# Output projection in an attention kernel: another set of seven products per four quadrants

## The chip, the cores and the metric

The kernel runs on one core of a Trainium2 chip. The core has a matrix engine (TensorE, "PE" in the profile, with its weight loads as "PEld"), a vector engine (VectorE, "DVE"), an activation engine (ScalarE, "ACT"), a general engine (GpSimd, "POOL") and a queueing engine (SyncE, "SP"). Transfers are issued from the queues of SP and ACT and carried by 16 DMA engines. The metric is device time in microseconds (us). The kernel before takes 888.16 us, the median of 3 runs (887.34 to 888.82).

## The reference

The input is `x`, 2048 rows of 640. It is layer-normed, and two branches work on the result.

- Branch A is attention with 32 heads of 192, over the last 512 positions of a K and a V cache: `q = xn @ wq`, a softmax over the scores, the weighted sum of V, and the output projection `o @ wo`, where `o` is 2048 x 6144 and `wo` is 6144 x 640.
- Branch B is a gated feed-forward: `(silu(xn @ w_gate) * (xn @ w_up)) @ w_down`, followed by another silu; call it `g`.

The result is `x + (o @ wo) * g`.

## The kernel before, in words

The program has three stages, written out by hand: each engine carries out its instructions in the order in which the code issues them (`tc.manual_schedule()`).

**First stage (0 to about 170 us).** Layer norm and branch B. `g` is stored to DRAM in `g_d`. Beside this, VectorE prepares `wo`: it is read in pieces (`wo_pieces`), sums of quadrants of it are formed in fp16 (`wo_sums`, L360) and stored to `wo_d` (L362).

**Second stage (about 170 to 698 us).** Attention, in 16 pairs of heads, about 33 us each. One pair is two halves; each half is a phase of scores (8 calls of `scores`, with the next q products between them) and a stretch of `pv`. ScalarE takes the exponential of each score tile (L651); score tiles have two buffers. V of a pair has one buffer, `V_p`, so its load (L181) can start only after the `pv` of the pair before, and the first `pv` of the new pair waits for it. The output of a pair is divided, transposed by DMA (L718) and stored to `o_d` in DRAM (L727). `beside(pr, n)` hangs further work at step `n` (0 to 15) of pair `pr`; the table `AHEAD` lists what is fetched for the third stage: `load_b` fetches the prepared operand of a product (always on ACT's queue here, L760, 128 x 7680 elements of 2 bytes), `load_a` fetches quadrants of `o`, and `wo_part` (L739, SP's queue) copies a bare quadrant of `wo` from DRAM to DRAM into `wo_d`, a quarter at a time, so that a later `load_b` reads it in long runs.

**Third stage (698 us to the end).** The output projection. Two row tiles of 128 make a row pair (`ROW_PAIRS`, 8 of them, number `n`). Per pair the left operand has four quadrants (two row tiles by two halves of the 6144), and `wo` has four (two halves of the 6144 by two halves of the 640 columns). The four result quadrants are formed from seven products instead of eight, by Strassen's method: `A_OF` and `B_OF` say which quadrants each product's operands are summed from. `a_sum` forms a sum on VectorE (L789); its three buffers rotate, two under the tag `qT` and one in the pool `late[0]`; the sum after next but one is issued after the product that used its buffer. `product` (L796) runs 24 matmuls of 128 x 320 into a PSUM bank. `run(n, m)` issues a product and then what takes its result out of PSUM: copies on ScalarE (L853, L868), sums on VectorE (`total`, L835), `finish` (L818, L819), which multiplies by `g` and adds `x`, and `store` (L823). `ORDER` runs the first two row pairs product by product in turn, and the other six one after the other. `load_xg` (L805, L806) fetches `x` and `g` of a pair. The loads and stores of this stage stand in SP's queue in program order.

Before the third stage starts, ACT's queue holds, in this order: the last divisions of the attention, one `load_b` (L760) into the pool `late[0]`, and then the first copies out of PSUM.

Of the kernel before, what the change touches and what calls it, by code (L numbers as in the profile page):

```python
# [10 lines left out]
ALU = mybir.AluOpType  # L11
# [4 lines left out]
def kernel(  # L16
# [66 lines left out]
    def mm_tile(which=None):  # L83
# [14 lines left out]
    M6, M3, M1, M5, M4, M2, M7 = PRODUCTS = range(7)  # L98
    A_OF = {
        M1: (0, 3, ALU.add), M2: (2, 3, ALU.add), M3: (0,), M4: (3,), M5: (0, 1, ALU.add),  # L100
        M6: (2, 0, ALU.subtract), M7: (1, 3, ALU.subtract),
    }
    B_OF = {
        M1: (B11, B22, ALU.add), M2: (B11,), M3: (B12, B22, ALU.subtract), M4: (B21, B11, ALU.subtract),
        M5: (B22,), M6: (B11, B12, ALU.add), M7: (B21, B22, ALU.add),
    }
    B_SUMS = [m for m in PRODUCTS if len(B_OF[m]) == 3]
    B_PARTS = [m for m in PRODUCTS if len(B_OF[m]) == 1]
# [3 lines left out]
    wo_d = dram.tile([len(PRODUCTS), P, KH, HC], h16, name="wo_d")  # L112
# [115 lines left out]
    with ExitStack() as fctx:  # L228
# [119 lines left out]
        def wo_sums(n, ks):  # L348

            t = won[n]  # L350
            if not ks.start:
                won["sums"] = ffw.tile([P, len(B_SUMS), 2, HC], h16, name="wo_s")
            sums = won["sums"]

            def piece(q):
                return t[:, q[0], :, q[1] * HC : (q[1] + 1) * HC]

            for k in ks:
                x, y, op = B_OF[B_SUMS[k]]
                nc.vector.tensor_tensor(sums[:, k, :, :], piece(x), piece(y), op)  # L360
            if ks.stop == len(B_SUMS):
                nc.sync.dma_start(  # L362
                    out=wo_d[0 : len(B_SUMS), :, 2 * n : 2 * n + 2, :].rearrange("s p c d -> p s c d"), in_=sums[:, :, :, :]
                )
# [371 lines left out]
    def wo_part(m, c0, c1):  # L736

        k, n = B_OF[m][0]
        nc.sync.dma_start(  # L739
            out=wo_d[len(B_SUMS) + B_PARTS.index(m), :, c0:c1, :].bitcast(bf),  # L740
            in_=wo[(k * KH + c0) * P : (k * KH + c1) * P, n * HC : (n + 1) * HC].rearrange(
                "(c p) d -> p c d", p=P
            ),
        )

    def load_b(m, pool=None, eng=nc.scalar):
        if m in b_w:
            pass
        elif pool is None:
            flat = xc[:, 0:3, :, :].rearrange("p s c n -> p (s c n)")  # L750
            b_w[m] = flat.bitcast(bf).rearrange("p (c d) -> p c d", d=HC)
        else:
            b_w[m] = b_tile(m, pool)[:, :, :]
        if eng is None:
            return
        if m in B_SUMS:
            src = wo_d[B_SUMS.index(m), :, :, :]
        else:
            src = wo_d[len(B_SUMS) + B_PARTS.index(m), :, :, :].bitcast(bf)
        eng.dma_start(out=b_w[m], in_=src)  # L760
# [22 lines left out]
    def a_sum(n, m):  # L783
        x, y, op = A_OF[m]
        third = len(a_s) % 3 == 2
        a_s[n, m] = (late[0] if third else qpool).tile(
            [P, KH, P], h16, name="a_s", tag="a_s" if third else "qT", bufs=1 if third else 2
        )
        nc.vector.tensor_tensor(a_s[n, m][:], a_q[n, x][:], a_q[n, y][:], op)  # L789
# [19 lines left out]
    NAMES = ("m3", "e1", "f1", "m4", "f2", "c21", "y0", "g1")  # L809

    def f_tile(name):
        return temps[:, NAMES.index(name), :]

    def finish(n, side, k, s):

        t, cols = xg[n, side], slice(k * HC, (k + 1) * HC)
        y = f_tile("y0")
        nc.vector.tensor_tensor(y, s, t[:, 1, cols], ALU.mult)  # L818
        nc.vector.tensor_tensor(t[:, 0, cols], y, t[:, 0, cols], ALU.add)  # L819
# [7 lines left out]
    IN_TURN = (M6, M3, M1, M5, M4, M2, M7)  # L827
    ORDER = [(n, m) for ms in ((M6, M3), (M1,), (M5,), (M4,), (M2,), (M7,)) for n in range(2) for m in ms]
    ORDER += [(n, m) for n in range(2, len(ROW_PAIRS)) for m in IN_TURN]
# [11 lines left out]
    def e1_tile(n):  # L841
        return f_tile("e1") if n % 2 == 0 else late[2][:, :]

    def run(n, m):

        ahead = n + 2 < len(ROW_PAIRS)
        if m == M6:
            product(n, M6, bank(n, "Y"))
        elif m == M3:
            Z = bank(n, "Z")  # L850
            product(n, M3, Z)
            acc[n, "m3"] = f_tile("m3" if n % 2 == 0 else "y0")
            nc.scalar.copy(acc[n, "m3"], Z)  # L853
        elif m == M1:
            S = bank(n, "S")
            product(n, M1, S)
            acc[n, "e1"] = e1_tile(n)
            total(acc[n, "e1"], S, acc[n, "m3"])
        elif m == M5:
            product(n, M5, acc[n, "Z"], first=False)  # L860
            acc[n, "f1"] = f_tile("f1" if n % 2 == 0 else "g1")
            total(acc[n, "f1"], acc[n, "e1"], acc[n, "Z"], ALU.subtract)
            finish(n, 0, 1, acc[n, "Z"])
        elif m == M4:
            X = bank(n, "X")
            product(n, M4, X)
            acc[n, "m4"] = f_tile("m4" if n % 2 == 0 else "m3")
            nc.scalar.copy(acc[n, "m4"], X)  # L868
            for q in (0, 2) if ahead else ():
                load_a(n + 2, q)  # L870
        elif m == M2:
            S = bank(n, "S")
            product(n, M2, S)
            f2, c21 = f_tile("f2"), f_tile("c21")
            total(f2, acc[n, "e1"], S, ALU.subtract)
            total(c21, S, acc[n, "m4"])
            total(f2, acc[n, "Y"], f2)
            finish(n, 1, 0, c21)
            finish(n, 1, 1, f2)
            store(n, 1)  # L880
            for q in (1, 3) if ahead else ():
                load_a(n + 2, q)
        else:
            X, f1, t = acc[n, "X"], acc[n, "f1"], xg[n, 0]
            product(n, M7, X, first=False)
            if (n, m) != ORDER[-1]:
                total(f1, X, f1)
                finish(n, 0, 0, f1)
                store(n, 0)
            else:  # L890
                total(f1, f1, t[:, 1, 0:HC], ALU.mult)
                total(f1, f1, t[:, 0, 0:HC])
                store(n, 0, slice(HC, D))
                total(f_tile("f2"), X, t[:, 1, 0:HC], ALU.mult)
                total(t[:, 0, 0:HC], f_tile("f2"), f1)
                store(n, 0, slice(0, HC), nc.scalar)
            if ahead:
                load_xg(n + 2)
# [20 lines left out]
    def beside(pr, n):  # L919
# [23 lines left out]
        (1, 10): (load_b, M6, pre), (4, 10): (load_b, M3, pre), (7, 10): (load_b, M1, pre),  # L943
# [5 lines left out]

    for k, m in enumerate(B_PARTS):  # L950
        for n in range(4):
            AHEAD[2 + 3 * k + n // 2, (7, 15)[n % 2]] = (wo_part, m, n * KH // 4, (n + 1) * KH // 4)
# [35 lines left out]
    load_b(M4, wide, None)  # L988
# [9 lines left out]
    for name in LAST.split():  # L998
# [7 lines left out]
        elif name == "2b1":  # L1006
            load_a(0, 3, new)
            load_a(1, 3, new)
            load_b(M4)
# [14 lines left out]
    late.append(late[0].tile([P, HC], f32, name="e1"))  # L1024
    load_b(M7, late[0], None)
    a_sum(*A_SUMS[2])
    load_b(M2, late[0])
    load_xg(0)
    load_xg(1)
    load_b(M7, eng=nc.sync)  # L1030
# [32 lines left out]
```

## Time and profile before

The profiled execution took 887.44 us, of which the span between the first and the last instruction is 885.6 us. The clock granted to TensorE is 1.0, full speed, throughout.

| | us |
|---|---|
| Median of 3 runs | 888.16 |
| Profiled execution / its span | 887.44 / 885.6 |
| TensorE busy, whole span | 875.5 (99%) |
| VectorE busy | 599.1 (68%) |
| ScalarE busy | 404.1 (46%) |
| TensorE busy from 698 to 881 us (third stage) | 182.92 of 183.00 |
| VectorE busy in the same stretch | 116.17 |
| DMA engines, mean busy share, in the same stretch | 0.57 |
| DMA engines, mean busy share, 170 to 698 us | 0.85 |

Busy time of TensorE counts matmuls whose ends are modelled, so the idle time of an engine between two instructions, and what ended it, tells more than the share. In a line of the timeline the columns are the start, the duration, the engine, the line of code, the operation, output and inputs, the count, and in brackets the idle time before it with what ended it. "SPq" and "ACTq" are a queue's own instructions: the time in which it hands over a transfer, not the transfer itself.

### The profile page before, as it was taken

The numbers are of one execution on the slowest core, as the hardware profiler recorded it, in microseconds if no ns is written. First come the engines' busy times: TensorE is split into PE (matmuls) and PEld (weight loads), VectorE is DVE, ScalarE is ACT, GpSimd is POOL, SyncE is SP. The second block draws the span as 40 slices with busy tenths as digits, with TensorE's granted clock in tenths as the row PEclk, the third lists the DMA queues.
The fourth block names the chain that finished last, engine by engine and source line by source line (L and its number), as shares of the span: only waits on it lengthen the run. The fifth ranks groups of instructions, "written<-read, shape, count | busy, mean of one in ns | idle before, by whom it ended". The sixth has DMA issues, their size and how long they took to land.

```text
span 885.6 us, 22930 instructions
## 1 busy us (share of the span) xinstructions
PE 875.5 (99%) x9705; PEld 581.0 (66%) x9705; DVE 599.1 (68%) x1020; ACT 404.1 (46%) x577; POOL 114.1 (13%) x215
## 2 busy tenths in 40 slices
PE   9999999999999999999999999999999999999997
PEld 6455555567667666766766766766766777777775
DVE  6464786177777776777867777877875467666664
ACT  4222222466666666666666666666667300000000
POOL 0000001012132132132132132132120000000000
PEclk9999999999999999999999999999999999999999
DMA  9669877247999979979878777979799998655420
GB/s 296 166 183 273 212 222 226 66 69 175 231 199 212 182 164 254 193 165 213 228 156 190 157 155 174 195 145 218 160 208 278 221 346 297 216 173 181 171 69 16
DMA packets 271494, 169.44 MB, mean 191 GB/s; under 512 B 174112, under 2 KB 266400, under 8 KB 270496
## 3 DMA queue, kind: packets, MB, share of 16 engines
q1 hardware_dynamic: 269456, 154.12, 72.3%
q10 hardware_dynamic: 1936, 13.86, 4.3%
q8 instruction: 76, 1.25, 0.6%
q14 instruction: 26, 0.21, 0.1%
HBM read 91.91 MB, written 44.17 MB: 154 GB/s over the span
## 4 chain that ended last, share of the span: by engine, by line
PE 95%; DMA 2%; DVE 2%; issue 1%; ACTq 0%; ACT 0%; SPq 0%
PE acc L796 19%; PE sc L647 18%; PE mm L593 12%; PE sc L369 11%; PE mm L686 10%; PE sc L686 9%; PE mm L579 8%; PE mm L390 6%; DMA V_p<-in_A_v_cache_dram 1%; PE mm L402 1%; DMA x_t<-in_A_x_dram 1%; PE gu L369 0%; DMA xnT<-xn 0%; DVE a_s L789 0%; DVE xc L835 0%
## 5 line engine op out<-in xcount | busy, mean ns | idle before, releaser
L651 ACT ACTIVATE p_t<-sc 128x1024 bf16<-128x1024 f32 x256 | 253.7, 1024 | 59.9 <-PE sc L647 55.5
L647 PE MATMUL sc<-qT,khat 64*128 64x512 bf16 x1536 | 198.0, 376 | 0.0
L686 PEld LDWEIGHTS <-p_t 64*128 64x128 bf16 x4096 | 172.8, 94 | 11.6 <-DMA V_p<-in_A_v_cache_dram 2.0
L647 PEld LDWEIGHTS <-khat 64*128 64x128 bf16 x1536 | 89.0, 94 | 75.1 <-issue 0.3
L796 PEld LDWEIGHTS <-a_s 128*128 128x128 f16 x960 | 93.8, 98 | 36.9 <-DVE a_s L789 0.6
L686 PE MATMUL mm<-V_p,p_t 64*128 64x193 bf16 x2112 | 112.2, 243 | 2.3 <-DMA V_p<-in_A_v_cache_dram 2.3
L796 PE MATMUL acc<-b_w,a_s 128*128 128x320 f16 (+1 forms) x768 | 107.1, 299 | 0.1
L686 PE MATMUL sc<-V_p,p_t 64*128 64x193 bf16 x1984 | 104.8, 243 | 0.0
L584 DVE TENSOR_REDUCE qT<-mm 128x512 bf16<-128x1024 f32 x66 | 80.6, 1223 | 29.7 <-PE mm L579 27.2
L593 PE MATMUL mm<-xc,wq_p 64*128 64x512 f16 x750 | 94.4, 376 | 0.0
L593 PEld LDWEIGHTS <-wq_p 64*128 64x128 f16 (+1 forms) x1050 | 58.6, 94 | 47.6
L631 POOL TENSOR_TENSOR m_f<-m_f 128x1024 f32<-128x1024 f32 x28 | 65.8, 2351 | 178.0 <-DVE qT L626 178.0
L715 ACT ACTIVATE O_b<-sc,r 128x192 bf16<-128x192 f32 x120 | 44.0, 420 | 89.7 <-PE sc L686 80.3
L579 PE MATMUL mm<-xnT,wq_p 64*128 64x512 bf16 x660 | 82.9, 376 | 0.5 <-DVE qT L584 0.5
L789 DVE TENSOR_TENSOR a_s<-a_q 128x3072 f16<-128x3072 bf16 x40 | 69.3, 1750 | 7.1 <-issue 7.1
L369 PE MATMUL sc<-xnT,wg_sb 128*128 128x512 bf16 (+1 forms) x260 | 60.2, 354 | 1.4 <-DMA xnT<-xn 1.1
L579 PEld LDWEIGHTS <-wq_p 64*128 64x128 bf16 x660 | 36.1, 94 | 36.8 <-issue 5.7
L369 PE MATMUL sc<-xnT,wu_sb 128*128 128x512 bf16 (+1 forms) x260 | 60.3, 354 | 0.0
L377 DVE TENSOR_TENSOR hT<-sc,sg 128x512 bf16<-128x512 f32 x46 | 31.5, 687 | 42.4 <-ACT sg L376 42.2
L376 ACT ACTIVATE sg<-sc 128x512 bf16<-128x512 f32 x46 | 27.3, 596 | 69.7 <-PE sc L369 69.7
L704 DVE RECIPROCAL r<-mm 128x4 f32<-128x4 f32 x66 | 12.0, 183 | 68.2 <-PE mm L686 68.1
L626 DVE TENSOR_TENSOR qT<-mm,m_f 128x1024 bf16<-128x1024 f32 x30 | 36.7, 1225 | 31.6 <-ACT m_f L623 31.6
(82 smaller groups left out, 860.3 us busy)
## 6 DMA issues: line engine op xcount, KB each, us to landing
o_d<-OT_b SPq DMA_DIRECT2D x64, 384.0 KB, 5.9
a_q<-o_d SPq DMA_DIRECT2D x28, 768.0 KB, 6.1
wo_d<-wo_s SPq DMA_DIRECT2D x12, 800.0 KB, 4.8
b_w<-wo_d ACTq DMA_DIRECT2D x5, 1920.0 KB, 9.9
won<-in_A_wo_dram SPq DMA_DIRECT2D x24, 320.0 KB, 5.4
wq_rows<-in_A_wq_dram SPq DMA_DIRECT2D x16, 480.0 KB, 4.6
wq_rows<-in_A_wq_dram SPq DMA_DIRECT2D x30, 240.0 KB, 6.0
K_p<-in_A_k_cache_dram SPq DMA_DIRECT2D x32, 192.0 KB, 6.7
```

Source lines behind the costliest of these rows:

```text
L369: nc.tensor.matmul(out, w_sb[:, c, f * P : (f + 1) * P], xnT[:, c, qc], start=(c == 0), stop=(c == NC - 1),)
L390: nc.tensor.matmul(dn[:, n, 0:HC], hTs[b][:, f, rows], wd_sb[:, f, n * HC : (n + 1) * HC], start=(f == 0), stop=(f == NF - 1),)
L579: nc.tensor.matmul(q_ps[:, h, :], w[r, AS_IS[j], c, :], xnT[r, c, b * 512 : (b + 1) * 512], start=(c == 0), stop=(c == NC - 1),)
L584: nc.vector.reduce_sum(q_of(i, j), q_ps[:, :, :].rearrange("p h n -> p n h"), axis=AX.X)
L593: nc.tensor.matmul(ps[:, h, :], ws[h][r, c, :], xs[h][r, c, :], start=(first and c == 0), stop=(c == NC - 1), skip_group_check=True,)
L631: eng.tensor_tensor(m_f[:, SIDE_S, :, :], diag, m_f[:, SIDE_S, :, :], ALU.subtract)
L647: nc.tensor.matmul(sc[:, h, :], khat[r, j, ks], q_of(i, j)[r, :], start=(j == 0), stop=(j == 2))
L651: nc.scalar.activation(p_t[:, :, :], sc[:, :, :], ACT.Exp, scale=scale)
L686: m = nc.tensor.matmul(acc[:, k, h * 256 : h * 256 + Dh + 1], Ps[i][kc][r, h, qt * P : (qt + 1) * P], V_p[r, kc, h, 0 : Dh + 1], start=(p ...
L715: nc.scalar.activation(O_b[:, qt, h, :], a_k[:, h, 0:Dh], ACT.Copy, scale=r[:, k, h, :])
L789: nc.vector.tensor_tensor(a_s[n, m][:], a_q[n, x][:], a_q[n, y][:], op)
L796: nc.tensor.matmul(ps[k] if ns > 1 else ps, at[:, c, :], b_w[m][:, c, k * w : (k + 1) * w], start=(first and c == 0), stop=(c == KH - 1), ...
```

## The change

The seven products are formed by another scheme with four operand sums on each side instead of five, where sums are built on one another: on the left A11-A21, A21+A22, (A21+A22)-A11 and A12-((A21+A22)-A11), and on the right likewise. The products are run in the order M1, M7, M2, M5, M6, M4, M3. Three of the four result quadrants are added up in PSUM: M2 is accumulated on M1's bank, M4 on M7's, M3 on M5's, after the first product's value has been copied or summed out of the bank (M1 and M7 by a copy on ScalarE, M5 by a sum on VectorE). Bare quadrants of `wo` are now the right operands of three products, M1, M2 and M3. M1's and M2's are loaded straight from `wo` into SBUF, in runs of 320 elements (3072 of them), on ACT's queue at steps (1, 10) and (7, 10); M3's is copied to `wo_d` by four `wo_part` in pairs 2 and 3; the other four `wo_part`, in pairs 5 and 6, are gone. In the very last product the quadrant's partial sum is multiplied by `g` and added to `x` before the product, as it was before, but for another quadrant. The loads of the next left quadrants move: A11 and A21 after M6, A22 after M4, A12 after M3 and thus behind a store. Number and size of matmuls stay the same.

```diff
-    M6, M3, M1, M5, M4, M2, M7 = PRODUCTS = range(7)
+    A11, A12, A21, A22 = range(4)
+    M1, M7, M2, M5, M6, M4, M3 = PRODUCTS = range(10, 17)
     A_OF = {
-        M1: (0, 3, ALU.add), M2: (2, 3, ALU.add), M3: (0,), M4: (3,), M5: (0, 1, ALU.add),
-        M6: (2, 0, ALU.subtract), M7: (1, 3, ALU.subtract),
+        M1: (A11,), M2: (A12,), M4: (A22,),
+        M7: (A11, A21, ALU.subtract), M5: (A21, A22, ALU.add), M6: (M5, A11, ALU.subtract),
+        M3: (A12, M6, ALU.subtract),
     }
     B_OF = {
-        M1: (B11, B22, ALU.add), M2: (B11,), M3: (B12, B22, ALU.subtract), M4: (B21, B11, ALU.subtract),
-        M5: (B22,), M6: (B11, B12, ALU.add), M7: (B21, B22, ALU.add),
+        M1: (B11,), M2: (B21,), M3: (B22,),
+        M7: (B22, B12), M5: (B12, B11), M6: (B22, M5), M4: (B21, M6),
     }
...
+    def wo_part(c0, c1):
+        nc.sync.dma_start(out=wo_d[len(B_SUMS), :, c0:c1, :].bitcast(bf), in_=wo_quarter(M3, c0, c1))
...
         if m in B_SUMS:
             src = wo_d[B_SUMS.index(m), :, :, :]
+        elif m == M3:
+            src = wo_d[len(B_SUMS), :, :, :].bitcast(bf)
         else:
-            src = wo_d[len(B_SUMS) + B_PARTS.index(m), :, :, :].bitcast(bf)
+            src = wo_quarter(m)
         eng.dma_start(out=b_w[m], in_=src)
...
-    ORDER = [(n, m) for ms in ((M6, M3), (M1,), (M5,), (M4,), (M2,), (M7,)) for n in range(2) for m in ms]
-    ORDER += [(n, m) for n in range(2, len(ROW_PAIRS)) for m in IN_TURN]
+    ORDER = [(n, m) for ms in ((M1, M7), (M2,), (M5,), (M6,), (M4,), (M3,)) for n in range(2) for m in ms]
+    ORDER += [(n, m) for n in range(2, len(ROW_PAIRS)) for m in PRODUCTS]
...
     def run(n, m):
         ahead = n + 2 < len(ROW_PAIRS)
...
+        u, v, c = (f_tile(n, k) for k in range(3))
+        if m == M1:
+            ps = bank(n, "M1+M2")
+            product(n, M1, ps)
+            nc.scalar.copy(u, ps)
+        elif m == M7:
+            ps = bank(n, "M7+M4")
+            product(n, M7, ps)
+            nc.scalar.copy(v, ps)
+        elif m == M2:
+            ps = acc[n, "M1+M2"]
+            product(n, M2, ps, first=False)
+            finish(n, 0, 0, ps, in_psum=True)
+            if (n, M3) == ORDER[-1]:
+                store(n, 0, slice(0, HC))
         elif m == M5:
+            ps = bank(n, "M5+M3")
+            product(n, M5, ps)
+            total(v, ps, v)
+        elif m == M6:
+            ps = bank(n, "M6")
+            product(n, M6, ps)
+            total(u, ps, u)
+            total(v, u, v)
+            finish(n, 1, 1, v)
+            for q in (A11, A21) if ahead else ():
+                load_a(n + 2, q)
         elif m == M4:
+            ps = acc[n, "M7+M4"]
+            product(n, M4, ps, first=False)
+            total(c, ps, u)
+            finish(n, 1, 0, c)
             store(n, 1)
+            if ahead:
+                load_a(n + 2, A22)
         else:
+            ps, t, last_cols = acc[n, "M5+M3"], xg[n, 0], slice(HC, D)
+            if (n, m) == ORDER[-1]:
+                total(u, u, t[:, 1, last_cols], ALU.mult)
+                total(u, u, t[:, 0, last_cols])
+            product(n, M3, ps, first=False)
+            if (n, m) == ORDER[-1]:
+                total(c, ps, t[:, 1, last_cols], ALU.mult)
+                total(t[:, 0, last_cols], c, u)
+                store(n, 0, last_cols, nc.scalar)
             else:
+                total(u, ps, u)
+                finish(n, 0, 1, u)
+                store(n, 0)
             if ahead:
+                load_a(n + 2, A12)
                 load_xg(n + 2)
...
-        (1, 10): (load_b, M6, pre), (4, 10): (load_b, M3, pre), (7, 10): (load_b, M1, pre),
+        (1, 10): (load_b, M1, pre), (4, 10): (load_b, M7, pre), (7, 10): (load_b, M2, pre),
...
-    for k, m in enumerate(B_PARTS):
-        for n in range(4):
-            AHEAD[2 + 3 * k + n // 2, (7, 15)[n % 2]] = (wo_part, m, n * KH // 4, (n + 1) * KH // 4)
+    for n in range(4):
+        AHEAD[2 + n // 2, (7, 15)[n % 2]] = (wo_part, n * KH // 4, (n + 1) * KH // 4)
...
-    late.append(late[0].tile([P, HC], f32, name="e1"))
-    load_b(M7, late[0], None)
+    load_b(M3, late[0], None)
     a_sum(*A_SUMS[2])
-    load_b(M2, late[0])
+    load_b(M4, late[0])
     load_xg(0)
     load_xg(1)
-    load_b(M7, eng=nc.sync)
+    load_b(M3, eng=nc.sync)
```

## Prediction

> **What bounds the kernel.** First view: busy time by stretch. The columns after the length are busy us (and instructions) of PE, PEld, DVE, ACT and POOL, then the granted clock, the DMA share and GB/s.
>
> ```profile
> 170.00:698.00 528.00, 525.28 (x7351) 356.04 (x7348) 383.45 (x656) 347.98 (x475) 107.04 (x198) 1.00 0.85 187
> 698.00:881.00 183.00, 182.92 (x1349) 131.34 (x1344) 116.17 (x153) 8.14 (x20) 0.00 (x0) 1.00 0.57 190
> ```
>
> In the stage that is rewritten TensorE is idle for 0.08 of 183 us, while VectorE works 116 and ScalarE 8. The 1344 matmuls follow one another every 183/1344 = 136 ns, so one product of 24 takes 3.26 us, and 8 x 7 of them 182.8. The change keeps all of them. Work taken off VectorE is therefore worth nothing by itself; only waits of TensorE, and the piece after the last matmul, can move. So the second view is what TensorE waited for in the whole span:
>
> ```profile
> PE mm L686 <- DMA V_p<-in_A_v_cache_dram: 2.3, 4, 0.9
> PE gu L290 <- DVE zero_t L236: 1.2, 1, 1.2
> PE sc L369 <- DMA xnT<-xn: 1.1, 1, 1.1
> ```
>
> Only the first can be touched by this change: `V_p` comes late in three pairs, and each time the pair before held a 1.9 MB `load_b`. Third, the timeline of the queues where the stages meet and at the end, and of SP with and without a `load_b` beside it:
>
> ```profile
> 711.17 6.68 PE L796 MATMUL acc<-b_w,a_s 128*128 128x320 f16 x48
> 711.06 0.33 ACTq L760 DMA_DIRECT2D b_w<-wo_d  x1
> 711.43 0.75 ACT L853 COPY xc<-acc 128x320 f32<-128x320 f32 x2 [11.17 <-PE acc L796]
> 722.08 0.49 DVE L818 TENSOR_TENSOR xc<-acc,xg 128x320 f32<-128x320 f32 x1 [0.44 <-DMA xg<-g_d]
> ...
> 881.07 1.01 DVE L835 TENSOR_TENSOR xc<-xc,xg 128x320 f32<-128x320 f32 x2
> 882.00 0.48 DVE L835 TENSOR_TENSOR xc<-acc,xg 128x320 f32<-128x320 f32 x1
> 882.51 0.49 DVE L835 TENSOR_TENSOR xg<-xc 128x320 bf16<-128x320 f32 x1
> 883.04 0.34 ACTq L823 DMA_DIRECT2D out_dram<-xg  x1
> ```
>
> ```profile
> 228.21 0.34 ACTq L760 DMA_DIRECT2D b_w<-wo_d  x1
> 228.28 1.03 ACT L651 ACTIVATE p_t<-sc 128x1024 bf16<-128x1024 f32 x1
> 229.52 1.02 ACT L651 ACTIVATE p_t<-sc 128x1024 bf16<-128x1024 f32 x1 [0.21 <-PE sc L647]
> ...
> 229.59 4.12 SPq L136 DMA_DIRECT2D K_p<-in_A_k_cache_dram  x2
> 233.75 4.45 SPq L727 DMA_DIRECT2D o_d<-OT_b  x2
> ...
> 251.09 0.51 PE L686 MATMUL mm<-V_p,p_t 64*128 64x193 bf16 x8
> 251.78 0.51 PE L686 MATMUL mm<-V_p,p_t 64*128 64x193 bf16 x8 [0.18 <-DMA V_p<-in_A_v_cache_dram]
> ...
> 363.56 1.29 SPq L136 DMA_DIRECT2D K_p<-in_A_k_cache_dram  x2
> 364.90 2.33 SPq L727 DMA_DIRECT2D o_d<-OT_b  x2
> ```
>
> The first copies out of PSUM stood behind the `load_b` at 711.06, although the product that the first one drains had long ended. At the end VectorE, not TensorE, was late. And beside a `load_b` SP needs 8.6 us for what takes 3.6 without.
>
> **The change, part by part.** The profiled run took 887.44 us, 1.8 more than its span and 0.7 less than the median of 888.16; I sum differences against the run and put them on the median.
>
> *Sums.* On the left 40 sums of 1.75 us become 32 (14 us of VectorE gone), on the right 12 of 60 at 0.48 go (5.8 us), and 12 stores to `wo_d` shrink by a fifth. All lay beside TensorE: 0. If the chained sums came late, they would cost, so I check the tightest. The first `finish` now follows the fifth product instead of the seventh; it waits for `xg`, which landed at about 722 in this run, so VectorE stands from 714 on. Queued behind it are a second `finish` (its `g` lands about 1.7 us later, from the queue's order), the sum out of M5's bank, and M6's second operand, done at about 723.7 + 1.0 + 0.5 + 1.75 = 727.0. TensorE wants that at its tenth product, 698.1 + 9 x 3.26 = 727.5, plus the stall found next, 728.3. Cover: 1.3 us; 0.
>
> *First product.* M6 waited 0.18 us for its sum at 698.12; M1 takes a bare quadrant: up to -0.15, swallowed by the next item.
>
> *M2 on M1's bank.* M2, fifth in turn, is due at 711.1 and must wait until ScalarE has copied M1's value. That copy stands behind `load_b` in ACT's queue, which nothing in the change moves: issue at 711.06, copy from 711.43 for 0.43 (the row's copies), so M2 starts at 711.9. Before, the fifth product had a bank of its own and started at 711.17. Cost +0.8, all on the path; bounds 0 (issue 0.8 us earlier) and +1.5. The next three copies follow within 1 us and are needed 3.3 us later at the earliest: 0. From the third pair on a copy has a whole product (3.26 us) to end: 0.
>
> *One stall in mid-stage.* Two gaps of weight loads before sums (0.6 us in all) are the 0.18 above and about 0.25 near 743.6, at the third pair's first sums. Its first product now needs no sum, and the second's (M7) is ready some 10 us ahead: -0.25 (0 to -0.4).
>
> *Loads moved on SP.* A12 of the next pair but one is now issued behind a store. Tightest for the third pair: the store can go at about 743 (M3 ends at 741.3, three VectorE operations of 0.49), the load lands 6.0 us later by its median, at 749.4; M2 wants it at 751. Cover 1.6 us; 0. The slowest of these loads (13.3 us, one of four handed over together) would cost 5.7.
>
> *The end.* Before, after the last but one product VectorE had 9 operations to do and began the final one at 882.00, while the last product had ended so that it could have begun at 881.15 (877.89, the same step one product earlier, plus 3.26). Now five operations of 0.49 follow the last but one product, 2.5 us in a product of 3.26, so the final one starts on time: -0.85 (0 to -0.9).
>
> Third stage: +0.8 - 0.25 - 0.85 = -0.3 us.
>
> *Two column loads on ACT's queue.* M1's and M2's operand was one run per partition (128 runs, 0.33 us to hand over) and is now 3072 runs. No row has such a transfer. Handing over: lowest 0.33; SP's one of 1536 runs (`wd_sb`) took 1.09, twice that is 2.2; the worst of `wo_part`, the same columns, took 2.6. I take 1.1 to 2.2, by the row nearest in size. Behind it on ACT wait the exponentials: at 228.2 ScalarE is still busy with one until 229.3, the next can only start at 229.5 when its scores are there, and TensorE needs that one's buffer about 0.4 us after its end. So up to 1.3 + 0.4 = 1.7 us is hidden, and the excess is paid by TensorE, twice: by the middle of my estimate 0; bounds 0 and 2 x 0.9 = +1.8.
>
> *What they do to SP.* Per MB, the queues' shares in the profile give q10 (large runs) 609 engine-us / 13.86 = 44 and q1 (mixed, small) 10245 / 154 = 66. A load of 1.97 MB takes 5.4 us of all 16 engines now, and at most 8.1 in small runs: up to +2.7 us of transfer in pairs 1 and 7. `V_p` of pairs 2 and 8 came 0.36 and 0.67 us too late for TensorE (eight `pv` matmuls take 0.33 us, but after those at 251.09 and 451.41 the next start at 251.78 and 452.41). If SP falls back by the whole 2.7, they cost 2 x 2.7 more; if small runs let SP's transfers through, they vanish, -1.03. I take 0, between the two: the only rows, 4.12 against 1.29, are for long runs. [...]
>
> *`wo_part`.* Four copies go in pairs 5 and 6, where no `V_p` was late by them (pair 5's came 2 us late at 350, before its `wo_part` at 350.88): 0.
>
> Sum: -0.3. On the median: 888.16 - 0.3 = 887.9 us.
>
> **Rivals.** (a) *The column loads hold ACT or SP, and it is slower.* For it: a queue beside a `load_b` took 4.12 and 4.45 us for two transfers, so handing over can stretch. Against: `wd_sb`'s 1.09 with the engines full. It decides from a hand-over of 2.8 us each: 2 x (2.8 - 1.7) - 0.3 = +1.9, 890.1; at 3.8 each, near the stretch of SP's two hand-overs (4.12), it is +3.9, 892.1. (b) *All small gains come, and more:* M2's copy is not late (-0.8), `V_p` is in time (-1.03): -0.3 - 0.8 - 1.03 = -2.1: 886.0. For it: both waits hang on transfers of a few us that can shift. Against: nothing in the diff touches the order on ACT. (c) *VectorE's relief is the gain:* some 20 us; the 0.08 us of idle TensorE speaks against it, 2%.
>
> **How the numbers follow.** About 0.2%, 1.8 us, is what a measurement of this kernel can tell from no change. Forecast, within it: 0.58. Rival (a), slower: 0.28. Rivals (b) and (c), faster: 0.12 and 0.02. Range: from (b) less 0.5 us of scatter of the runs, 885.5, to just short of (a)'s 892.1: 891.8.
>
> **What will show it.** Right, if the fifth product of the third stage starts 0.7 to 1 us behind a pace of 3.26 us per product with ScalarE's copy just before it, if the final VectorE operation starts within 0.25 us of the last product's end, and if ACT's issue of the two column loads is below 1.7 us. Wrong, if that issue stretches over an exponential and TensorE waits for score buffers near 230 and 430 us, if `V_p` waits sum to more than 4 us, or if a product waits for a chained sum or for A12 near 728 and 751 us.

## The result and the profile after

The changed kernel takes 889.95 us (median of 20 runs, 888.36 to 893.45), the kernel before 888.03 beside it (20 runs, 886.59 to 890.57). The ratio is 1.0026 with a 95% interval of 1.0017 to 1.0036: slower by about 2 us, just beyond what can be told from no change. The prediction was 887.9, no change.

The profiled execution took 888.36 us with a span of 886.6, 0.92 more than the profiled one of before (887.44). What TensorE waited for in the whole span (total, times, longest, in us):

```profile
PE mm L689 <- DMA V_p<-in_A_v_cache_dram: 4.2, 5, 1.6
PE gu L291 <- DVE zero_t L237: 1.2, 1, 1.2
PE mm L582 <- DVE qT L587: 0.5, 1, 0.5
```

`V_p` is again the largest wait, and it has grown from 2.3 to 4.2 us; the line counts only what stands directly ahead of a matmul. The whole pause shows in the starts of successive matmuls: what lies between two starts, less what lies between the same two in run 9 below, where `V_p` is never late (0.20 us from the last score matmul to the first `pv`). I call that *the pauses at `V_p`* from here on. They fall in three places, always in the pair after an early `load_b`:

| pause at `V_p`, us, in pair | 2 | 5 | 8 | sum |
|---|---|---|---|---|
| early load in the pair before: before / after | M6 / M1 | M3 / M7 | M1 / M2 |  |
| before | 0.40 | 1.95 | 0.67 | 3.0 |
| after | 2.37 | 1.55 | 1.49 | 5.4 |

The expectations of the runs below speak of 3.1 and 5.7 us: they were written with a usual distance that is 0.1 us too short.
All growth is in pairs 2 and 8, those behind the two loads that now come straight from columns of `wo`; pair 5, behind a load of the old kind, has none. The timeline shows how. First SP's queue ahead of pair 2 in the kernel before, behind the lines at 229.59 and 233.75 that the prediction shows (start, length, queue, line, transfer):

```profile
238.30 7.12 SPq L718 DMA_TRANSPOSE OT_b<-O_b  x4
245.80 1.55 SPq L191 DMA_TRANSPOSE KT<-K_p  x1
247.45 1.67 SPq L181 DMA_DIRECT2D V_p<-in_A_v_cache_dram  x2
```

The same stretch in the kernel after, with the column load on ACT's queue and TensorE:

```profile
227.81 0.39 ACTq L764 DMA_DIRECT2D b_w<-in_A_wo_dram  x1
229.18 1.46 SPq L137 DMA_DIRECT2D K_p<-in_A_k_cache_dram  x2
230.68 3.78 SPq L730 DMA_DIRECT2D o_d<-OT_b  x2
237.09 10.07 SPq L721 DMA_TRANSPOSE OT_b<-O_b  x4
247.53 1.27 SPq L192 DMA_TRANSPOSE KT<-K_p  x1
248.90 1.72 SPq L182 DMA_DIRECT2D V_p<-in_A_v_cache_dram  x2
249.99 0.83 PE L650 MATMUL sc<-qT,khat 64*128 64x512 bf16 x6
252.39 0.51 PE L689 MATMUL mm<-V_p,p_t 64*128 64x193 bf16 x8 [1.58 <-DMA V_p<-in_A_v_cache_dram]
```

Read it from the top. Handing the column load over takes 0.39 us, hardly more than the 0.34 of a load in long runs. `K_p` passes quickly beside it, 1.46 us against 4.12. But the transfer lasts: the issue table has it land 15.7 us after its issue, the loads in long runs after 9.4 (9.9 before):

```profile
b_w<-wo_d ACTq DMA_DIRECT2D x3, 1920.0 KB, 9.4
b_w<-in_A_wo_dram ACTq DMA_DIRECT2D x2, 1920.0 KB, 15.7
```

So it runs from 227.8 to 243.6 and lies over the four transposes that stand next in SP's queue. They take 10.07 us in place of 7.12, and `V_p`, last in that queue, is handed over at 248.90 instead of 247.45, while TensorE in this run is some 0.4 us earlier than in the other (first `pv` of the stage at 184.66, not 185.08) and so asks for it earlier.

The third stage does what it should. Here is its fifth product, M2, which must wait until M1 has been copied out of their bank, and then the end:

```profile
712.30 0.33 ACTq L764 DMA_DIRECT2D b_w<-wo_d  x1
712.67 0.43 ACT L854 COPY xc<-acc 128x320 f32<-128x320 f32 x1 [10.55 <-DMA OT_b<-O_last]
713.14 3.15 PE L804 MATMUL acc<-b_w,a_q 128*128 128x320 bf16 x22
...
882.86 0.49 DVE L841 TENSOR_TENSOR xc<-acc,xg 128x320 f32<-128x320 f32 x1 [0.79 <-PE acc L804]
883.39 0.49 DVE L841 TENSOR_TENSOR xg<-xc 128x320 bf16<-128x320 f32 x1
883.91 0.34 ACTq L830 DMA_DIRECT2D out_dram<-xg  x1
```

The stage starts at 699.95, and M2, the fifth product, at 713.14, which is 13.19 us later; in the kernel before, where the fifth product had a bank of its own, it is 13.05. So M2 is 0.14 late. The final VectorE operation now waits for the last product, as the bracket says, and not the product for VectorE. From the start of the first matmul of the stage to that of the last, before took 182.69 us and after 182.57; from there to the end of the span 4.79 and 4.05. That is 0.86 us gained.

Sum for the two profiled executions: up to the first `pv` -0.4 (a wait near 34 us takes 0.43 us in place of 1.24, and earlier waits give half of that back; among the experiments below, run 3 left aside, the first `pv` starts between 184.1 and 185.7, so this is not the change's), pauses at `V_p` +2.4, third stage -0.86: +1.1, measured +0.92.

The median differs by 1.92, a microsecond more. Nine of the 20 executions of after have a mean granted clock of 1.000, and their median is 889.23; the other eleven have 0.996 to 0.999 and take 889.8 to 893.5. What that is, a later experiment's profile shows.

### The profile page after: what moved, and what is told of

It is laid out like the page before. It is cut to its first block, busy times and chain, and to the rows that moved or that the text cites. A ratio compares the mean times of both kernels' runs of the same rounds, so it can differ in the third digit from the quotient of the medians.

```text
span 886.6 us, 22883 instructions
## 1 busy us (share of the span) xinstructions
PE 876.1 (99%) x9705; PEld 581.4 (66%) x9705; DVE 581.4 (66%) x992; ACT 404.0 (46%) x577; POOL 113.9 (13%) x215
## 4 chain that ended last, share of the span: by engine, by line
PE 97%; DMA 2%; DVE 1%; issue 0%; ACTq 0%; SPq 0%
PE acc L804 21%; PE sc L650 18%; PE mm L596 13%; PE sc L372 11%; PE mm L689 10%; PE sc L689 9%; PE mm L582 8%; PE mm L393 6%; DMA V_p<-in_A_v_cache_dram 1%; PE mm L405 1%; DMA x_t<-in_A_x_dram 1%; PE gu L372 0%; DVE wq_p L174 0%; DVE qT L587 0%; ACTq L249 0%
## 5 line engine op out<-in xcount | busy, mean ns | idle before, releaser
L804 PEld LDWEIGHTS <-a_s 128*128 128x128 f16 x768 | 75.1, 98 | 29.2
L804 PE MATMUL acc<-b_w,a_q 128*128 128x320 bf16 (+1 forms) x576 | 81.8, 299 | 0.0
L804 PE MATMUL acc<-b_w,a_s 128*128 128x320 f16 (+1 forms) x576 | 81.8, 299 | 0.0
L804 PEld LDWEIGHTS <-a_q 128*128 128x128 bf16 x576 | 56.3, 98 | 22.1 <-issue 0.3
L854 ACT COPY xc<-acc 128x320 f32<-128x320 f32 x8 | 3.4, 428 | 141.3 <-PE acc L804 130.8
```

The source lines that it names most:

```text
L804: nc.tensor.matmul(ps[k] if ns > 1 else ps, at[:, c, :], b_w[m][:, c, k * w : (k + 1) * w], start=(first and c == 0), stop=(c == KH - 1), ...
```

## Experiments

Two theories at the start. *A*: the two column loads make `V_p` late, by way of SP's queue; the rest of the change is worth a little gain. *B*: the new form costs in the third stage (M2 behind the copy, the moved loads, the chained sums), and the time is lost there. Every run below was timed beside the kernel before on the same chip; all results stand in one table.

| run | pauses at `V_p`, us | time, us (lowest to highest) | before beside it | ratio (95%) |
|---|---|---|---|---|
| after | 5.4 | 889.95 (888.36–893.45) | 888.03 | 1.0026 (1.0017–1.0036) |
| 1 after, no column loads | 3.2 | 887.71 (885.54–889.58) | 887.34 | 1.000 (0.999–1.0011) |
| 2 before, with column loads | 5.6 | 891.06 (888.55–891.85) | 887.34 | 1.0037 (1.0023–1.0051) |
| 3 before, padded operands | 6.0, of it 0.3 in pair 11 | 897.50 (896.80–898.54) | 887.34 | 1.0116 (1.010–1.0131) |
| 4 after, quarters | none | 884.01 (882.74–884.69) | 887.34 | 0.996 (0.9948–0.9972) |
| 5 before, quarters | none | 883.94 (883.62–884.57) | 886.77 | 0.997 (0.9958–0.9981) |
| 6 after, `V_p` ahead of the keys | 1.5 | 884.29 (883.57–885.40) | 886.77 | 0.9975 (0.9966–0.9984) |
| 7 after, loads at step 2 | 12.7 | 899.98 (898.78–900.51) | 886.77 | 1.015 (1.0136–1.0164) |
| 8 after, quarters and `V_p` ahead | none | 883.15 (882.73–883.91) | 886.77 | 0.9963 (0.9951–0.9976) |
| 9 after, loads at step 7 | none | 882.92 (882.08–883.64) | 886.57 | 0.9951 (0.9936–0.9965) |
| 10 before, loads at step 7 | 0.3 in pair 11 | 883.86 (883.68–885.17) | 886.57 | 0.9967 (0.9955–0.998) |

### 1. The new form without column loads

M1's, M2's and M3's quadrants are copied to `wo_d` by twelve `wo_part`, and the three early loads fetch sums, in long runs. M1 and M2 go to other places in SBUF and are loaded later.

```diff
-        (1, 10): (load_b, M1, pre), (4, 10): (load_b, M7, pre), (7, 10): (load_b, M2, pre),
+        (1, 10): (load_b, M7, pre), (4, 10): (load_b, M5, pre), (7, 10): (load_b, M6, pre),
...
-    for n in range(4):
-        AHEAD[2 + n // 2, (7, 15)[n % 2]] = (wo_part, n * KH // 4, (n + 1) * KH // 4)
+    for k, m in enumerate(B_PARTS):
+        for n in range(4):
+            AHEAD[2 + 3 * k + n // 2, (7, 15)[n % 2]] = (wo_part, m, n * KH // 4, (n + 1) * KH // 4)
```

> The changed kernel without its two column loads: M7, M5 and M6, which lie in wo_d in one run per partition, are fetched at (1,10), (4,10) and (7,10); the bare operands M1, M2 and M3 are copied ahead by wo_part (12 copies), M1 is fetched at (14,14) and M2 just before the third stage. Nothing of the result changes. Theory A (the column loads hold SP's transfers up, V_p comes late): TensorE's waits for V_p fall from 4.2 us to about the 2.3 of before, and the time to about 0.3 us under before, 887.7 (887.2 to 888.4). Theory B (the new third stage costs the time, by M2's wait for ScalarE's copy or by chained sums): time stays within 0.5 us of the changed kernel's, about 890. If M2's wait is real when the third stage starts in time, the fifth product starts 0.5 to 0.9 us behind its pace.

Measured: 887.71, ratio 1.000; the loss is gone. The gain of the new form doesn't show in this median: four of the 11 executions have a mean clock of 0.998 and take 888.1 to 889.6 us. It shows in the profiled execution, whose span is 884.8, 0.8 below that of before. The lines of its timeline that answer to those above:

```profile
229.51 3.82 SPq L138 DMA_DIRECT2D K_p<-in_A_k_cache_dram  x2
...
237.42 7.87 SPq L722 DMA_TRANSPOSE OT_b<-O_b  x4
245.67 2.40 SPq L193 DMA_TRANSPOSE KT<-K_p  x1
248.18 1.24 SPq L183 DMA_DIRECT2D V_p<-in_A_v_cache_dram  x2
```

The old picture is back: `K_p` slow, the transposes short, `V_p` earlier. Its third stage, from the first matmul's start to the last's, takes 182.59 us, and its end 4.05, as in the kernel after. B falls: the whole new third stage is in this kernel and it isn't slower.

### 2. The old form with column loads

In the kernel before, M5 and M2, which need bare quadrants, are loaded straight from `wo` at the same two places; the copies to `wo_d` go on but are not read. M6, M1 and M4, which give up places to them, are fetched later.

```diff
-            src = wo_d[len(B_SUMS) + B_PARTS.index(m), :, :, :].bitcast(bf)
+            src = wo_quarter(m)
...
-        (1, 10): (load_b, M6, pre), (4, 10): (load_b, M3, pre), (7, 10): (load_b, M1, pre),
+        (1, 10): (load_b, M5, pre), (4, 10): (load_b, M3, pre), (7, 10): (load_b, M2, pre),
```

> The kernel before with only the column loads of the change: the bare operands M5 and M2 are fetched straight from wo in 3072 runs at (1,10) and (7,10), and the operands that stood there go to the places that become free; all eight wo_part stay, and nobody reads what they write. Products, sums and their order are those of before. Theory A: V_p waits rise from 2.3 to about 4.2 us and the time by 2 to 3 us, to about 890.5. Theory B: no change, 888.0 within 0.5.

Measured: 891.06, 3.7 us above before, with nothing of the new form in it. Timeline, the same stretch:

```profile
229.32 1.66 SPq L136 DMA_DIRECT2D K_p<-in_A_k_cache_dram  x2
...
237.43 9.68 SPq L718 DMA_TRANSPOSE OT_b<-O_b  x4
247.49 1.27 SPq L191 DMA_TRANSPOSE KT<-K_p  x1
248.86 1.81 SPq L181 DMA_DIRECT2D V_p<-in_A_v_cache_dram  x2
```

These are close to the lines of the kernel after, within 0.4 us. The pauses are 5.6 us, 2.6 more than before. The rest is the clock. This profile has a mean of 0.997, and busy time by stretch finds where (length, PE, PEld, DVE, ACT, POOL, granted clock, DMA share, GB/s):

```profile
251.00:252.00 1.00, 0.15 (x2) 0.00 (x0) 0.77 (x1) 0.75 (x1) 0.00 (x0) 1.00 0.86 180
252.00:253.00 1.00, 0.26 (x8) 0.27 (x9) 0.00 (x0) 0.27 (x1) 0.00 (x0) 1.00 1.08 320
253.00:254.00 1.00, 0.75 (x16) 0.60 (x14) 0.00 (x0) 0.00 (x0) 0.00 (x0) 0.88 1.08 355
254.00:255.00 1.00, 1.00 (x16) 1.00 (x14) 0.00 (x0) 0.00 (x0) 0.10 (x1) 0.50 1.03 288
255.00:256.00 1.00, 1.00 (x17) 1.00 (x14) 0.00 (x0) 0.00 (x0) 0.10 (x1) 0.50 0.93 259
256.00:258.00 2.00, 2.00 (x40) 2.00 (x36) 1.23 (x4) 0.00 (x0) 0.00 (x0) 0.71 0.43 136
```

Right behind the pause at `V_p` TensorE is granted half its clock for 3.4 us; the parts missing from 1.00 add up to 0.12 + 0.5 + 0.5 + 2 x 0.29 = 1.7 us. The hundredth `pv` matmul of this stretch is late by 1.6 us more than the pauses alone make it. With the 2.6 us that is 4.2, the difference between the spans of the two profiled executions (889.8 and 885.6). Most of the pause is thus paid a second time.

### 3. Many runs, but not out of `wo`

Is it the reading of `wo`, or the number of runs? In the kernel before, M6's and M1's operands, which are prepared sums, are stored a second time with gaps between the rows, and read from there in 3072 runs of 640 bytes.

```diff
+    PADDED = (M6, M1)
+    wo_p = dram.tile([len(PADDED), P, KH, 2 * HC], h16, name="wo_p")
...
+                for k, m in enumerate(PADDED):
+                    nc.sync.dma_start(
+                        out=wo_p[k, :, 2 * n : 2 * n + 2, 0:HC], in_=sums[:, B_SUMS.index(m), :, :]
+                    )
...
+        if m in PADDED:
+            src = wo_p[PADDED.index(m), :, :, 0:HC]
```

> The kernel before, with the operands M6 and M1 also stored in a second place with gaps (rows of 640 elements of which 320 are used), and fetched from there at (1,10) and (7,10): 3072 runs of 640 bytes, but not out of wo. It separates the number of runs from the place that they come from; the 24 more stores lie in the first stage. If the runs are the cause: V_p waits and time as in the changed kernel, about +2 to +3 us, 890.5. If it is the reading of wo in half rows: as before, 888.0 within 0.6.

Measured: 897.5, more than either theory gave. The waits of TensorE say why:

```profile
PE mm L692 <- DMA V_p<-in_A_v_cache_dram: 4.4, 5, 2.5
```

The loads land 16.1 us after issue, and the pauses are 6.0 us: at this step the number of runs is enough, whatever is read. But the 24 additional stores made the first stage wait too (4.2 us of TensorE for VectorE's `hT`, which was not in the other profiles; the first `pv` starts at 192.2), so the time of this run is no measure of the loads. The trace settles the question; the time does not.

### 4. The column loads in quarters

Back to the kernel after. Its three early loads are cut in four and handed over at steps 7 and 15 of pairs 4 to 9.

```diff
+    def load_part(m, c0, c1):
+        if m not in b_w:
+            b_w[m] = b_tile(m, pre)[:, :, :]
+        src = wo_d[B_SUMS.index(m), :, c0:c1, :] if m in B_SUMS else wo_quarter(m, c0, c1)
+        nc.scalar.dma_start(out=b_w[m][:, c0:c1, :], in_=src)
...
-        (1, 10): (load_b, M1, pre), (4, 10): (load_b, M7, pre), (7, 10): (load_b, M2, pre),
...
+    for k, m in enumerate((M1, M7, M2)):
+        for n in range(4):
+            AHEAD[4 + 2 * k + n // 2, (7, 15)[n % 2]] = (load_part, m, n * KH // 4, (n + 1) * KH // 4)
```

> The changed kernel with the three early operands fetched in quarters (480 KB each, ACT's queue) at steps 7 and 15 of pairs 4 to 9 instead of whole at step 10 of pairs 1, 4 and 7; M1 and M2 still straight from wo. Theory A, with the place and size of the load as the lever: no load is under way when SP readies V_p, V_p waits fall under 0.8 us, the time to 885 (884.3 to 886.0), under both kernels. If any traffic of short runs makes V_p late wherever it stands, waits stay at 2 us or more and the time at 888 to 890. Theory B: about 890.

Measured: 884.01, below both kernels. No wait for `V_p` is left in the trace. This gains more than undoing the change's harm, since the three pauses of the kernel before are gone as well.

### 5. The same quarters in the kernel before

If that is so, the kernel before must gain from it too.

```diff
-        (1, 10): (load_b, M6, pre), (4, 10): (load_b, M3, pre), (7, 10): (load_b, M1, pre),
...
+    QUARTERS = {}
+    for k, m in enumerate((M6, M3, M1)):
+        for n in range(4):
+            QUARTERS[4 + 2 * k + n // 2, (7, 15)[n % 2]] = (load_part, m, n * KH // 4, (n + 1) * KH // 4)
```

> The kernel before, its three early loads (M6, M3, M1, whole at step 10 of pairs 1, 4 and 7) fetched in four quarters each on ACT's queue, at steps 7 and 15 of pairs 4 to 9, as the quarters of the kernel after were; nothing else. If whole loads at step 10 are what makes V_p late in the kernel before too, its three pauses (3.1 us together) go: 884.5 to 885.5. The kernel after with quarters then stands 0.5 to 1 us below it, which is what the new form is worth in the third stage by the traces (its products take 182.6 us for 182.7, its end 4.1 us for 4.8). If the quarters gain by something that only the new form has, this one stays at 887 to 888; if the new form is worth nothing by itself, this one comes out at 884.0 too.

Measured: 883.94, ratio 0.997, no pause at `V_p`. It gains 2.8 us on the kernel before, close to its 3.0 us of pauses. Runs 4 and 5 were not timed together, so the two forms are compared by ratio, 0.996 against 0.997, whose intervals overlap: this run alone doesn't tell what the new form is worth. Runs 9 and 10 do better.

### 6. `V_p` ahead of the keys on SP's queue

The three whole column loads stay. Only the order of two transfers on SP is turned.

```diff
             if n == 0:
+                load_v(pr)
                 transpose_k(pr + 1)
...
-        if n == 0:
+        if n == 0 and pr == last:
             load_v(pr)
```

> The kernel after with one edit: on SP's queue the load of V_p stands ahead of the transpose of the next pair's keys, not behind it. The three whole loads stay as they are. If V_p is late because it is issued late on SP's queue, it comes earlier by what that transpose took there (1.3, 2.6 and some 1.3 us in the three places), and the pauses at V_p (1.85+0.63, 1.30+0.36, 1.26+0.35 = 5.7 us) shrink to 1 to 2.5 us together: 885 to 887. If V_p is late because its own data come in slowly behind the column load's, the place on the queue matters little, the pauses stay above 4 us and the time at 889 to 890.

Measured: 884.29, better than expected. Timeline and wait of this kernel:

```profile
238.16 10.70 SPq L721 DMA_TRANSPOSE OT_b<-O_b  x4
249.32 1.24 SPq L182 DMA_DIRECT2D V_p<-in_A_v_cache_dram  x2
250.61 1.92 SPq L192 DMA_TRANSPOSE KT<-K_p  x1
```

```profile
PE mm L689 <- DMA V_p<-in_A_v_cache_dram: 1.0, 2, 0.6
```

The transposes of `OT_b` are still stretched, to 10.7 us. `V_p` comes as early as its queue lets it, the pauses shrink from 5.4 to 1.5 us, and no timed run has a mean clock below 0.999. The gain over after, in ratio 0.5%, is some 4.5 us, the 3.9 of the pauses and a part of the clock's. So the harm of the loads at step 10 runs through SP's queue, not through `V_p`'s own data: ahead of pair 2 the two halves of `V_p` land 2.9 and 3.4 us after their issue here, 3.4 and 3.2 in the kernel after, and 3.6 and 3.2 in the kernel before.

### 7. The whole loads at step 2

Are they harmless earlier, clear of the transposes of the pair's second half?

```diff
-        (1, 10): (load_b, M1, pre), (4, 10): (load_b, M7, pre), (7, 10): (load_b, M2, pre),
+        (1, 2): (load_b, M1, pre), (4, 2): (load_b, M7, pre), (7, 2): (load_b, M2, pre),
```

> The kernel after with its three whole loads issued at step 2 of pairs 1, 4 and 7 in place of step 10: the same transfers with the same short runs, some 10 to 15 us earlier, so that they are over (15.7 us from issue) before SP comes to the transposes that stand ahead of V_p. If it is the meeting with those transposes that costs, the pauses at V_p go below 1 us and the time to 884 to 885.5. If the short runs cost wherever they stand (TensorE or ACT waits elsewhere, by the transposes of the pair's first half), other waits of 2 us or more take their place and the time stays at 887 to 890.

Measured: 899.98, 13 us above before: a miss by more than any other. I had looked only at `V_p` of the next pair. The timeline shows that ACT hands the load over 0.6 us ahead of the keys' transpose and 4 us ahead of `V_p` of the *same* pair:

```profile
210.97 0.39 ACTq L764 DMA_DIRECT2D b_w<-in_A_wo_dram  x1
211.59 3.37 SPq L192 DMA_TRANSPOSE KT<-K_p  x1
215.02 2.08 SPq L182 DMA_DIRECT2D V_p<-in_A_v_cache_dram  x2
```

Here, other than at step 10, it is above all `V_p`'s own data that come slowly: they land 7.0, 5.0 and 8.0 us after their issue in pairs 1, 4 and 7. TensorE's pauses there are 4.2, 2.9 and 5.5 us. Busy time by stretch around the first of these:

```profile
219.00:222.00 3.00, 0.00 (x0) 0.00 (x0) 0.00 (x0) 0.48 (x1) 0.00 (x0) 1.00 1.23 286
222.00:223.00 1.00, 0.78 (x16) 0.63 (x18) 0.00 (x0) 0.00 (x0) 0.00 (x0) 1.00 1.09 342
223.00:224.00 1.00, 1.00 (x20) 1.00 (x17) 0.00 (x0) 0.00 (x0) 0.10 (x1) 0.57 1.10 371
224.00:225.00 1.00, 1.00 (x17) 1.00 (x14) 0.00 (x0) 0.00 (x0) 0.10 (x1) 0.50 0.19 61
225.00:226.00 1.00, 1.00 (x17) 1.00 (x14) 0.15 (x1) 0.00 (x0) 0.00 (x0) 0.50 0.00 0
```

The clock falls to 0.50 at each of the three pauses, for 3.4 us again: behind the first, and already at the end of the other two (means of 0.92 from 323 to 326 us and of 0.93 from 427 to 432, then 0.50). Counted like the 1.6 us of run 2, I estimate that at 1.5 us each. 12.7 - 3.0 of pauses, 4.5 of clock and -0.86 of the third stage make +13.3; measured +13.2. A miss in its place, but the price of a late `V_p` comes out clearly.

### 8. Quarters and `V_p` ahead

> The kernel after with the quarters of the earlier run and the load of V_p ahead of the keys' transpose. With quarters no pause at V_p is left in the trace, so the theory gives nothing for this: 884.0, within 0.7 us. If V_p's place on the queue had a worth of its own, or the later keys cost something, it differs by more than 1 us.

Measured: 883.15, ratio 0.9963, against 0.996 for the quarters alone. The time is 0.86 us below the 884.0 expected, a little more than the 0.7 allowed, but the two runs were not timed together. By the ratios, where no pause is left, the order on SP is worth nothing that these runs can tell.

### 9 and 10. The whole loads at step 7, in both kernels

Step 7 comes some 5 us after SP has issued the pair's own `V_p`, and some 28 ahead of the next.

```diff
-        (1, 10): (load_b, M1, pre), (4, 10): (load_b, M7, pre), (7, 10): (load_b, M2, pre),
+        (1, 7): (load_b, M1, pre), (4, 7): (load_b, M7, pre), (7, 7): (load_b, M2, pre),
```

> The kernel after with its three whole loads at step 7 of pairs 1, 4 and 7, that is some 5 us after SP has issued V_p of the same pair and some 30 us ahead of V_p of the next, where the first quarter of the earlier run stood. At step 2 the load was handed over 4 us before SP issued V_p of its own pair, and made that one late by 3.9, 3.0 and 5.6 us. If what costs is a load that is running when SP has to bring the transposes and V_p across, this place costs nothing: no pause at V_p above 0.5 us, 883.5 to 885. If a whole load in short runs costs somewhere wherever it stands, the transposes of the pair's first half become late in its place and TensorE waits 2 us or more, 886 to 890.

```diff
-        (1, 10): (load_b, M6, pre), (4, 10): (load_b, M3, pre), (7, 10): (load_b, M1, pre),
+        (1, 7): (load_b, M6, pre), (4, 7): (load_b, M3, pre), (7, 7): (load_b, M1, pre),
```

> The kernel before with its three whole early loads at step 7 in place of step 10. If place alone decides, its pauses at V_p (3.1 us) go as they did with quarters: 884 to 885, and the new form at the same place stands 0.5 to 1 us below it, or less by what short runs cost over long ones there. If long runs, which hold SP's queue while they last but are over sooner (9.9 us), cost at step 7 too, it stays above 886.

Measured: 882.92 (run 9) and 883.86 (run 10). Run 9 is the fastest of all, and it differs from the kernel after in three digits. Busy time by stretch where the three pauses were, first the kernel after, then run 9:

```profile
249.00:255.00 6.00, 3.99 (x67) 2.72 (x65) 1.93 (x2) 2.05 (x2) 0.20 (x2) 1.00 1.03 255
350.00:356.00 6.00, 4.81 (x82) 3.39 (x78) 2.50 (x4) 2.17 (x3) 0.38 (x3) 1.00 0.90 238
451.00:457.00 6.00, 4.87 (x89) 3.66 (x86) 2.56 (x5) 2.05 (x2) 0.20 (x2) 1.00 0.80 230
```

```profile
249.00:255.00 6.00, 6.00 (x112) 4.80 (x108) 3.74 (x6) 2.60 (x3) 0.81 (x3) 1.00 0.90 263
350.00:356.00 6.00, 6.00 (x136) 5.67 (x134) 3.71 (x8) 1.78 (x4) 0.39 (x4) 1.00 0.20 42
451.00:457.00 6.00, 6.00 (x118) 4.97 (x114) 4.44 (x12) 2.35 (x7) 0.29 (x3) 1.00 0.42 53
```

TensorE, second column, was busy for 3.99, 4.81 and 4.87 of 6 us and is now busy throughout. The same transfers in the same short runs cost nothing here. SP's queue in run 9, with the load handed over at 218.8, and the landing of the column loads, tell why:

```profile
221.92 7.63 SPq L721 DMA_TRANSPOSE OT_b<-O_b  x4
...
237.90 6.04 SPq L721 DMA_TRANSPOSE OT_b<-O_b  x4
...
246.84 1.26 SPq L182 DMA_DIRECT2D V_p<-in_A_v_cache_dram  x2
```

```profile
b_w<-in_A_wo_dram ACTq DMA_DIRECT2D x2, 1920.0 KB, 9.3
```

The load stretches the four transposes that run beside it, 7.63 us against 6.01 in the kernel after, but no `V_p` stands right behind those. The ones that do have `V_p` behind them take 6.04 us. And the load itself is shorter: the two land 8.8 and 9.8 us after issue, the long-run loads at the same two places in run 10 after 7.3 and 8.5. Within run 9 the long-run load of pair 4 takes 9.2. So the number of runs costs 1.5 us of transfer at most here and 4.7 to 5.9 at step 10 (after against before, pairs 7 and 1); what it cost TensorE here went with whether the transfer still lasted when SP had to get the transposes and `V_p` across (pauses of 5.4 us at step 10, 12.7 at step 2, none at step 7).

Runs 9 and 10 were timed together, at the same place in both forms, and their times do not overlap (883.64 is the highest of the one, 883.68 the lowest of the other): by the medians the new form is 0.94 us faster. The traces of before and after gave 0.86 us for the third stage, those of runs 9 and 10 give 0.99.

## Why the prediction was wrong, point by point

- **The step that failed: "What they do to SP. ... I take 0, between the two."** The two bounds were -1.03 and 2 x 2.7; measured in the trace is +2.8 for the two pairs (2.37 - 0.40 and 1.49 - 0.67), above the middle of that span (2.2), +2.4 with pair 5; against run 1, the new form without column loads, it is +2.2 in all. I had the place, the queue and the late transfer, named a `V_p` above 4 us as the sign of it, and then set the cost to the harmless value because the only rows were for long runs. The trace of before spoke clearly on one half: `V_p` was already late behind each early load. With a lateness already there, SP's later hand-over of `V_p` was paid about in full. Ahead of pair 2 it came 1.45 us later, with TensorE 0.4 earlier, and the pause grew by 1.97; ahead of pair 8 it came 2.07 later, with TensorE 1.15 later from the pauses before, and the pause grew by 0.82. So the downward bound deserved little weight.
- **"At most +2.7 us of transfer" was too low a bound.** It shared the queue's time out per MB. From issue to landing the loads went from 9.9 to 15.7 us, +5.8. At step 7, with other transfers beside it, the difference is 1.5 us at most (runs 9 and 10), which the bound would have covered: among SP's transfers at step 10 a load in short runs took that much longer, and no share of the whole program's queue time told it.
- **Quick beside short runs, but for longer.** The bound of -1.03 asked that short runs let SP's transfers through. The hand-over of `K_p` bears it out, 1.46 and 1.66 us beside short runs (after, run 2) against 4.12 and 3.82 beside long ones (before, run 1). The bound was wrong all the same, because the load then lasts 6 us longer (15.7 against 9.9) and meets the next transfers in the queue, the four transposes, which take 10.07 us in place of 7.12. Why it lasts longer was not shown: at step 7 loads in the same short runs land at most 1.5 us later than those in long ones.
- **Handing over, 0: right,** for another reason. I had estimated 1.1 to 2.2 us and found it hidden up to 1.7; it took 0.39. The 3072 runs lengthen the hand-over by 0.06 us. Rival (a) names ACT or SP: its ACT leg, by which it was priced, is refuted; its SP leg is what happened. That the time, 889.95, came out just below its 890.1 is luck, since that price was worked out for ACT.
- **Off the account altogether: the clock.** That a pause at `V_p` can be followed by 3.4 us at half clock stood in no term. It accounts for 0.7 us of the median (889.95 against 889.23 for the executions at full clock). It isn't the new kernel's alone: of the 12 executions of before beside runs 9 and 10 one has a mean clock of 0.997, and it is the longest, 889.81. Run 2 shows it in a profile (0.50 behind the pause in pair 2); in the kernel after the profiled execution was one without it, so there it is inferred from the mean clocks of the timed runs.
- **M2 on M1's bank, +0.8: too high.** Measured +0.14 in the kernel after, and no wait in run 9, where the copy that M2 waits for ends at 707.80 and M2 starts on time at 708.41. I had taken the `load_b` ahead of the copies as fixed at 711.06. It isn't: it waits for the last transposes on SP, the first two of which took 5.83 us in the trace of before, and 3.15 and 2.73 in after and run 9. In before it came 12.9 us behind the start of the stage, in after 12.3, in run 9 11.6.
- **The end, -0.85: nearly right.** The final VectorE operation follows the last product directly; start of the last matmul to the end of the span went from 4.79 to 4.05, -0.74.
- **Mid-stage stall, -0.25: right;** none is left in after. **Sums 0, A12 0, `wo_part` 0:** no wait for any of them appears among TensorE's waits. For the third stage as a whole -0.3 became -0.86, and the runs at step 7 give -0.94.
- **Rival (b),** 886.0, was two effects; the one on ACT came nearly as it said, the one at `V_p` went the other way. **Rival (c):** VectorE's busy time fell from 599.1 to 581.4 us and is worth nothing visible, as said.

Put together, the change is two: a new form, worth 0.9 us, and two loads of another shape in an unlucky place, which cost 2.8 us of pauses, and 0.6 to 4.2 us more in the executions in which the clock drops (889.84 to 893.45 against 889.23).

## What to carry to other kernels

A transfer that "is prefetched anyway" is judged by what is in flight beside it when it still runs: list what the other queues must bring across between its issue and its landing, and which of these was already late. Before pricing a new load, look for a wait behind the old one; here the place of the old loads was already costing 3 us, and moving three loads by three steps was worth more than all the arithmetic saved. And where the one open term has bounds from a small gain to a large loss, and the resource is already late, don't take zero.

## What the runs showed of the hardware that I had not expected

- The hand-over of a 1.9 MB load takes 0.33 us with 128 runs and 0.39 with 3072. The transfer itself took 9.9 and 15.7 us in the surroundings of step 10 (medians of before and after), and 7.3 and 8.8 in those of step 7 (pair 1, runs 10 and 9).
- Ahead of pair 2, SP's hand-over of `K_p` took 4.12 us beside the load in long runs (before) and 1.46 beside the one in short runs (after); its four transposes, which come later, took 7.12 and 10.07. Ahead of pair 8 it is 4.78 and 1.44, and 6.89 and 8.79. Here the second delay cost more, since `V_p` stood behind the transposes.
- At a pause of TensorE of 1.8 us in run 2 (its longest wait for `V_p` is 1.6 in the trace), and at each of 2.9 us or more in run 7, the granted clock went to 0.50 for 3.4 us. It isn't strict: the pause of 1.8 us in the kernel after (longest wait 1.6 too) and one of 2.7 us in run 3 (longest wait 2.5) were followed by a clock of 1.00. What in the pause decides was not tried.
